# A DeltaNet and SwiGLU kernel: an order planned anew from other durations of computing steps

## The chip, the core and the metric

The kernel runs on one core of a Trainium2 chip, in fp32. A core has TensorE (PE: matmuls, with weight loads listed apart as PEld), VectorE (DVE), ScalarE (ACT), GpSimd (POOL), and SyncE (SP), which here issues nearly all DMAs. Matmul results go to eight PSUM banks of 128 partitions by 512 fp32 values. Counts of matmuls here are those of the profile, in which each fp32 matmul of the program is listed as two. The metric is the device time of one execution in microseconds. Before the change the median of 3 runs is 671.55 us (670.78 to 674.18).

## What is computed

Attention in the form of DeltaNet, then a root-mean-square norm and a SwiGLU feed-forward layer (FFN). There are 4 batches of 8 heads, 768 positions, head width 48; the FFN has 3072 tokens, width 384 and inner width 1536.

```python
k_n = k / (np.linalg.norm(k, axis=-1, keepdims=True) + 1e-06)
for t in range(S):                               # 768 steps
    kt, vt, bt = k_n[:, :, t], v[:, :, t], beta[:, :, t, None]
    y[:, :, t] = np.einsum('bhd,bhde->bhe', q[:, :, t], state)
    v_old = np.einsum('bhde,bhd->bhe', state, kt)
    state = state + bt[:, :, :, None] * np.einsum('bhd,bhe->bhde', kt, vt - v_old)
...
x = y.transpose(0, 2, 1, 3).reshape(B * S, H * D)
xn = x / np.sqrt(np.mean(x * x, axis=-1, keepdims=True) + 1e-06) * rms_g
g = xn @ w_gate
val = xn @ w_val
return (g / (1.0 + np.exp(-g)) * val) @ w_out
```

The weights arrive as float64 and are converted on the chip; the rest is fp32.

## The kernel before

**Tiling and stages.** The 768 positions are cut into 12 chunks of 64. Within a chunk the recurrence is solved for all 32 heads at once: a triangular system is inverted, and the state is carried from chunk to chunk. A chunk's 256 tokens (64 positions of 4 batches) then go through the norm and the FFN. For each chunk c there are these stages, by the names of the functions:

- `load`: q, k and v from DRAM by SP. For chunks from 2 on q comes in sixteen pieces.
- `norms`: lengths of k's rows (ACT, then DVE L729 and L730, POOL L731, DVE L734 and L735).
- `qpart`: q transposed, then products with k. In chunks 0 and 1 the transposition is done by PE; from chunk 2 on by one DVE instruction over 128x1024 (`square_turn`, L715). `scores` (L704) is 64 matmuls on 64 rows and 64 columns, into two banks; DVE masks them into pt (L765).
- `prep16` (chunks 0 and 1) and `invert` (from chunk 2 on): the inverse. `invert` reads products of k from DRAM into at (SP), scales them by beta (DVE L1023), sets up (ACT `start` L1028, `start2` L1034; DVE L1048, L1053, L1058), and does 15 steps of two DVE instructions each (L1070 and L1076), in which each needs the one before it. Then `spread` (ACT L1093, POOL L1096) and DMAs. `prep16` does the same for 16-wide blocks in 7 steps (L903 and L909).
- `recur`: state products (L1199, L1210), the difference from v (DVE L1246), the inverse times it (L1281, L1295, L1307, L1317; `u` is written by ACT L1349 and DVE L1351), the new state (L1404, DVE L1355), y (DVE L1439), the norm (ACT L1429, POOL `root` L1452 to L1455). From chunk 4 on y goes through DRAM and is transposed by DVE (L1473); before that by PE (L1483). DVE L1510 and L1522 form sums of xf.
- the FFN: chunks 0 and 1 by `ffn_plain` (up L1558, down L1540), the rest by `ffn` and `down`, which save multiplications: 30 groups of 8 matmuls up (L1651), each read from its bank by ACT (L1663) or added by DVE (L1661); Silu (ACT L1667) and a DVE product (L1668); then `down` with DVE sums (L1700), seven groups of 12 matmuls (L1708), and DVE and ACT to read them (L1713, L1717).

The conversion of the 18 pieces of weights (ACT, then DVE L607, L610, L615, L639) takes place in the first 100 us, beside chunks 0 to 2.

**Who sets the order.** All instructions are first listed as `Op`s by `P.add(engine, duration, function, priority, r=, w=, ...)`. The duration is a number in us in the source, such as `1.0` or `V(n) = 0.13 + 0.0011 * n`. `Plan.forward` then lays the operations out on five engines from these durations (it also has terms for banks, DMA service, and the supply of instructions); `backward` gives each one its latest start; `shake` shifts priorities at random, from one number. `run` does `rounds` plain rounds and then one for each number in `MOVES`, and keeps the order whose planned end is the earliest. The operations are issued in that order, so it is fixed in the program:

```python
        for k in range(rounds + len(MOVES)):
            order = self.forward([t for t, _ in free], until if filler else 0.0)
            ...
            if best is None or self.end < best[0]:
                best = self.end, [(op, op.start) for op in order]
            if k >= rounds - 1:
                if k < rounds + len(MOVES) - 1:
                    self.shake(MOVES[k - rounds + 1])
                continue
            self.backward()
            self.reorder()
```

Each shake builds on the state that the one before it left. In planned gaps of PE before 70 us, `filler` puts matmuls of the identity into a spare bank (L1826), with 1, 2 or 4 blocks of 128 columns each. Banks are handed out in the planned order too. On the chip an engine takes its instructions in the program's order and waits by semaphores for other engines.

Of the kernel before, what the change touches and what calls it, by code (L numbers as in the profile page):

```python
# [25 lines left out]
ROUNDS, MOVES = (8, 3), (8000067, 8000597, 8000948, 8001017, 8002724, 8006360, 8008220, 8019300, 8029128, 8041120, 8046040, 8061420, 8103060, 8171660, 8171980, 8172520, 8176051, 8186548, 8187777, 8188940, 8197021, 8197169, 8200311, 8221546, 8225628, 8270861, 8283640, 8284428, 8285760, 8285870, 8288410, 8295221, 8301729, 8305291, 8310247, 8324080, 8458740, 8499977, 8522895, 8527737, 8540674, 8542770, 8573880, 8576584, 8577340, 8579620, 8580620, 8594840, 8603040, 8637560, 8655411, 8656870, 8664720, 8672920, 8873930, 8885129, 8893086, 8956398, 8960108, 9314698, 9382016, 9442358, 9601943)  # L26
BLOCK, ASKED, LACKED = 256, 140, 193
REACT, TURN, LAND = 2.4, 3.45, 2.6
STICK = 1.0
# [315 lines left out]
def kernel(  # L345
# [17 lines left out]
    nc = tc.nc  # L363
# [21 lines left out]
    half = sbt("half", [128, 16])  # L385
# [44 lines left out]
    AK = [("acc", 0), ("acc", 1)]  # L430
# [17 lines left out]
    ms = sbt("ms", [128, 2, 2], 2)  # L448
    rs = sbt("rs", [128, 2], 2)
# [333 lines left out]
    def prep16(c):  # L783
        pr = 8.0 if c == 1 else 0.0
        pd = pr + (1 if c else 0)
        pi = (1.0, 45.0)[c]
        i2, ikq = c, c
# [10 lines left out]
        psf = Group()  # L798
# [57 lines left out]
        ab = [("ab", c, n) for n in range(4)]  # L856
        ak = [("acc", c)]
# [15 lines left out]
                nc.scalar.copy(flat(side)[:, L * c : L * c + 33 * 15 + 1 : 33], share())  # L873

        P.add("ACT", 0.6, start, pd, r=["half"], w=ak)
        P.add("ACT", 0.4, start2, pd + 0.5, r=[psf], w=ak, last=psf)
        x, xkeys = x16[c], [("xs", c)]
        diag = a16[c].rearrange("p j t -> p (j t)")[:, 1 : 1 + 34 * 7 + 1 : 34]
        pair = x.rearrange("p i t -> p (i t)")[:, 0:128].rearrange("p (j k) -> p j k", k=L // 2)
# [17 lines left out]
        for j in range(0, L - 2, 2):  # L897
            n, m = j + 2, L - 2 - j

            def step(j=j, n=n, m=m):  # L900
                old, new, lo = (3, 0, 1) if j % 4 else (0, 3, 0)
                cols = slice(L * c + j + 2, L * c + L)
                nc.vector.tensor_tensor(  # L903
                    out=acc[:, 1:3, 0:n, cols].rearrange("p a i t -> p i a t"),
                    in0=sides[old][:, 0:n, j : j + 2, None].to_broadcast([128, n, 2, m]),
                    in1=a16[c][:, None, j : j + 2, j + 2 : L].to_broadcast([128, n, 2, m]),
                    op=ALU.mult,
                )
                nc.vector.tensor_reduce(  # L909
                    out=acc[:, new, 0:n, cols],  # L910
                    in_=acc[:, lo : lo + 3, 0:n, cols].rearrange("p a i t -> p i t a"),
                    axis=AXL.X,
                    op=ALU.add,
                )

            P.add("DVE", 0.47 + 0.0052 * n * m, step, pi, r=ab, w=ak)

        xflat = x.rearrange("p i t -> p (i t)")

# [5 lines left out]
                else:  # L925
                    nc.vector.tensor_copy(out=dst, in_=src)

        P.add("ACT" if c else "DVE", 0.97 if c else 0.55, spread, pi, r=ak, w=xkeys)
        P.add("DVE", V(256), lambda: nc.vector.transpose(out=turned[1], in_=xflat), pi, r=xkeys, w=["turn1"])
        psb = Group()  # L930

# [78 lines left out]
    def invert(c):  # L1010
        pd = due(c, 110) + 1
# [24 lines left out]
                        bt[rows, par : W : 2],  # L1036
                    )

        P.add("ACT", 1.0, start, pd, r=["half"], w=AK)
        P.add("ACT", 0.9, start2, pd + 0.5, r=bkeys, w=AK)  # L1040


# [22 lines left out]
        for j in range(0, W - 2, 2):  # L1065
            n, m = j // 2 + 1, W - 2 - j

            def step(j=j, n=n, m=m):
                old, new, lo = (3, 0, 1) if j % 4 else (0, 3, 0)
                nc.vector.tensor_tensor(  # L1070
                    out=acc[:, 1:3, 0:n, j + 2 : W].rearrange("p a i t -> p i a t"),
                    in0=acc[:, old, 0:n, j : j + 2, None].to_broadcast([128, n, 2, m]),
                    in1=at_[:, None, j : j + 2, j + 2 : W].to_broadcast([128, n, 2, m]),
                    op=ALU.mult,
                )
                nc.vector.tensor_reduce(  # L1076
                    out=acc[:, new, 0:n, j + 2 : W],
                    in_=acc[:, lo : lo + 3, 0:n, j + 2 : W].rearrange("p a i t -> p i t a"),
                    axis=AXL.X,
                    op=ALU.add,  # L1080
                )

            P.add("DVE", 0.47 + 0.0052 * n * m, step, pi, r=[("at", 0), ("at", 1)], w=AK)

        def spread(dst, op, turn):
            for side in range(2):
# [90 lines left out]
    def recur(c):  # L1177
# [245 lines left out]
        for h in halves:  # L1423
            gy = groups(psy, h)

            if c == 0:
                p = h[0]
                for g in range(2):
                    P.add("ACT", A(192) + 0.15, lambda p=p, g=g: nc.scalar.activation(  # L1429
                        out=xflat[:, 128 : 320], in_=psy[g, p].t[:, 192 * p : 192 * p + 192], func=ACTF.Square,  # L1430
                        scale=1.0 / math.sqrt(DM), accum_out=ms[i2][:, p, g : g + 1],
                    ), py, r=[psy[g, p]], w=[("x1", 1), ("ms", i2, p)], last=psy[g, p])
# [429 lines left out]
```

## Time and profile before

| What | Value |
|---|---|
| median of 3 runs | 671.55 us (670.78 to 674.18) |
| profiled execution | 673.21 us, of it span 671.5 us |
| mean granted clock of PE | 0.994 |
| matmuls and weight loads | 10070 each |
| L1651, all | 301.2 us busy, 276 and 277 ns each |
| L1661 (DVE) | 121.3 us, 180 times 683 ns |
| L1076, L1070 (DVE) | 70.9 and 52.7 us, 150 times each |
| L1028 (ACT, `start` of `invert`) | 10.4 us, 10 times 1041 ns |
| L715 (DVE, qt) | 12.4 us, 10 times 1238 ns |
| PE idle, 0 to 100 us of the span | 9.7 us |
| PE idle, 100 us to the end | below 1 us in the windows of 20 us |

Times are of one profiled execution. In the profile an engine's idle time ahead of a group is put down to the instruction that released it last. "PE bank L704 <- DVE qt L715" is time in which PE stood ahead of L704 and L715 on DVE, which writes qt, ended the wait. A row with "issue" is time for which the profile shows no cause. SPq is the time of SP's queue in issuing.

### The profile page before, as it was taken

The numbers are of one execution on the slowest core, as the hardware profiler recorded it, in microseconds if no ns is written. First come the engines' busy times: TensorE is split into PE (matmuls) and PEld (weight loads), VectorE is DVE, ScalarE is ACT, GpSimd is POOL, SyncE is SP. The second block draws the span as 40 slices with busy tenths as digits, with TensorE's granted clock in tenths as the row PEclk, the third lists the DMA queues.
The fourth block names the chain that finished last, engine by engine and source line by source line (L and its number), as shares of the span: only waits on it lengthen the run. The fifth ranks groups of instructions, "written<-read, shape, count | busy, mean of one in ns | idle before, by whom it ended". The sixth has DMA issues, their size and how long they took to land.

```text
span 671.5 us, 23512 instructions
## 1 busy us (share of the span) xinstructions
PE 657.3 (98%) x10070; PEld 608.2 (91%) x10070; DVE 577.0 (86%) x1199; ACT 298.2 (44%) x685; POOL 88.5 (13%) x105
## 2 busy tenths in 40 slices
PE   9899989999999999999999999999999999999997
PEld 6788768787799999999999999999999999999997
DVE  6999889999999998997998898899998798457472
ACT  7554343454235455355345345345345354343241
POOL 4212211050300040040031030030040010000000
PEclk9999979999999999999999999999999999999999
DMA  9483666573325336345347456476346434102100
GB/s 233 125 221 108 135 166 167 91 146 75 48 63 79 63 84 107 57 99 91 54 123 109 76 132 96 82 168 97 48 117 92 84 79 70 26 2 48 24 1 24
DMA packets 261822, 62.31 MB, mean 93 GB/s; under 512 B 248627, under 2 KB 253782, under 8 KB 261718
## 3 DMA queue, kind: packets, MB, share of 16 engines
q1 hardware_dynamic: 258438, 60.02, 45.5%
q8 instruction: 79, 1.29, 0.8%
q10 hardware_dynamic: 3280, 0.79, 0.6%
q14 instruction: 25, 0.20, 0.1%
HBM read 44.25 MB, written 16.52 MB: 91 GB/s over the span
## 4 chain that ended last, share of the span: by engine, by line
PE 79%; DVE 12%; SPq 3%; DMA 2%; issue 2%; ACT 1%; POOL 1%; DVEq 0%; POOLq 0%
PE bank L1651 36%; PE bank L1708 19%; PE bank L1558 7%; PE bank L1540 4%; PE bank L704 3%; PE bank L1199 3%; SPq L487 3%; PE bank L1281 1%; PE bank L1317 1%; DVE tmp L1661 1%; DVE acc L1076 1%; PE bank L685 1%; PE bank L1404 1%; PE bank L1124 1%; DVE acc L1070 1%
## 5 line engine op out<-in xcount | busy, mean ns | idle before, releaser
L1651 PE MATMUL bank<-xf,w_in 128*128 128x128 f32 x1440 | 177.4, 276 | 0.0
L1651 PEld LDWEIGHTS bank<-xf,w_in 128*128 128x128 f32 x1440 | 168.7, 192 | 0.8
L1661 DVE TENSOR_TENSOR tmp<-tmp,bank 128x512 f32<-128x512 f32 x180 | 121.3, 683 | 34.6 <-PE bank L1651 30.2
L1651 PE MATMUL bank<-xf,more 128*128 128x128 f32 x960 | 123.8, 277 | 0.0
L1651 PEld LDWEIGHTS bank<-xf,more 128*128 128x128 f32 x960 | 115.1, 192 | 0.9
L1663 ACT COPY tmp<-bank 128x512 f32<-128x512 f32 x120 | 69.0, 584 | 63.0 <-PE bank L1651 49.4
L1667 ACT ACTIVATE tmp<-tmp 128x256 f32<-128x256 f32 x120 | 50.1, 417 | 93.7 <-DVE tmp L1661 93.2
L1076 DVE TENSOR_REDUCE acc<-acc 128x30 f32<-128x90 f32 (+4 forms) x150 | 70.9, 472 | 5.2
L731 POOL TENSOR_TENSOR knrm<-ksum,half 128x16 f32<-128x16 f32 x12 | 35.5, 2960 | 274.5 <-DVE ksum L730 274.5
L1708 PE MATMUL bank<-wo_sb,hf 128*128 128x192 f32 x360 | 63.8, 329 | 0.0
L1708 PEld LDWEIGHTS bank<-wo_sb,hf 128*128 128x128 f32 x360 | 58.1, 190 | 0.5
L1070 DVE TENSOR_TENSOR acc<-acc,at 128x60 f32<-128x60 f32 (+4 forms) x150 | 52.7, 351 | 2.4
L1668 DVE TENSOR_TENSOR hf<-tmp 128x256 f32<-128x256 f32 x120 | 49.0, 418 | 5.5 <-ACT tmp L1667 4.7
L1540 PE MATMUL bank<-wo_sb,hf 128*128 128x384 f32 x96 | 35.2, 506 | 0.0
L1558 PE MATMUL bank<-xf,w_in 128*128 128x256 f32 x144 | 34.6, 387 | 0.0
L1558 PE MATMUL bank<-xp,w_in 128*128 128x256 f32 x144 | 33.4, 383 | 0.0
L1558 PEld LDWEIGHTS bank<-xp,w_in 128*128 128x128 f32 x144 | 26.8, 190 | 4.6 <-DVE more L1616 0.2
L1558 PEld LDWEIGHTS bank<-xf,w_in 128*128 128x128 f32 x144 | 26.4, 190 | 4.4 <-issue 0.2
L1713 ACT COPY tmp<-bank 128x192 f32<-128x192 f32 x30 | 9.5, 316 | 41.7 <-PE bank L1708 41.2
L1540 PEld LDWEIGHTS bank<-wo_sb,hf 128*128 128x128 f32 x96 | 18.3, 196 | 9.9 <-issue 0.6
L1096 POOL COPY acc<-acc 128x128 f32<-128x128 f32 x40 | 18.8, 500 | 63.1 <-DVE acc L1076 62.8
L1510 DVE TENSOR_TENSOR xf<-xf 128x256 f32<-128x256 f32 (+1 forms) x70 | 24.7, 381 | 2.5 <-ACT xf L1475 1.9
(198 smaller groups left out, 985.8 us busy)
## 6 DMA issues: line engine op xcount, KB each, us to landing
at<-dkk SPq DMA_DIRECT2D x20, 256.0 KB, 3.7
more<-in_moe_w_gate_dram SPq DMA_DIRECT2D x6, 768.0 KB, 7.6
vt<-in_v_dram SPq DMA_DIRECT2D x24, 192.0 KB, 4.0
k<-in_k_dram SPq DMA_DIRECT2D x23, 192.0 KB, 4.2
out_dram<-tmp SPq DMA_DIRECT2D x46, 96.0 KB, 2.2
more<-in_moe_w_val_dram SPq DMA_DIRECT2D x5, 768.0 KB, 8.4
more<-in_moe_w_out_dram SPq DMA_DIRECT2D x5, 768.0 KB, 5.5
dyn<-yn SPq DMA_DIRECT2D x16, 192.0 KB, 2.0
```

The source lines that it names most:

```text
L731: P.add("POOL", 2.95, lambda: nc.gpsimd.tensor_tensor(out=knrm[i2], in0=ksum[i2], in1=half, op=ALU.pow), pn, r=[("ksum", i2), "half"], w=[ ...
L1070: nc.vector.tensor_tensor(out=acc[:, 1:3, 0:n, j + 2 : W].rearrange("p a i t -> p i a t"), in0=acc[:, old, 0:n, j : j + 2, None].to_broadc ...
L1076: nc.vector.tensor_reduce(out=acc[:, new, 0:n, j + 2 : W], in_=acc[:, lo : lo + 3, 0:n, j + 2 : W].rearrange("p a i t -> p i t a"), axis=A ...
L1510: P.add("DVE", V(128 * n), lambda dst=dst, a=a, b_=b_, op=op: nc.vector.tensor_tensor(out=dst, in0=a, in1=b_, op=op), pxv, r=[("xp", 0)], ...
L1540: nc.tensor.matmul(po[p].t[:, 0:DM], hf[:, spot(f), 128 * p : 128 * p + 128], wo_sb[:, spot(f)], start=(f == f0), stop=(f == f1 - 1), skip ...
L1558: nc.tensor.matmul(ps.t[:, TOK * side : TOK * side + TOK], w_in[:, side, h_, 3 * t + i_, n : n + 128], x_[:, 2 * t : 2 * t + 2].rearrange( ...
L1651: nc.tensor.matmul(g.t[:, 128 * z : 128 * z + 128], fac[:, side, 128 * f : 128 * f + 128], xf[:, xs], start=(begin and z == 0), stop=False ...
L1661: P.add("DVE", V(512), lambda t=t, g=g: nc.vector.tensor_tensor(out=t, in0=t, in1=g.t, op=ALU.add), -1, r=[g], w=[tk], last=g)
L1663: P.add("ACT", A(512), lambda t=t, g=g: nc.scalar.copy(t, g.t), -1, r=[g], w=[tk], last=g)
L1667: P.add("ACT", A(256), lambda t=t: nc.scalar.activation(out=t[:, 0:256], in_=t[:, 0:256], func=ACTF.Silu), -1, w=[tk])
L1668: P.add("DVE", V(256), lambda t=t, f0=f0, p=p: nc.vector.tensor_tensor(out=hf[:, spot(f0) : spot(f0) + 2, 128 * p : 128 * p + 128], in0=t[ ...
L1708: nc.tensor.matmul(g.t[:, 0:192], a_[:, f], b_[:, f], start=(begin and f == 0), stop=(f == 5), skip_group_check=True)
```

## The change

Seven lines with durations of computing steps, the seed of the plain rounds (8 to 21) and their number (3 to 16), and the list of moves (63 to 92 numbers, none in common). No instruction's operands, shape or engine is changed, and no duration of a transfer. The number of instructions of each kind is the same on all engines but for the fillers.

```diff
-ROUNDS, MOVES = (8, 3), (8000067, 8000597, 8000948, 8001017, 8002724, ...
+ROUNDS, MOVES = (21, 16), (21000076, 21000207, 21000651, 21003860, 21005160, ...
...
         P.add("ACT", 0.6, start, pd, r=["half"], w=ak)
-        P.add("ACT", 0.4, start2, pd + 0.5, r=[psf], w=ak, last=psf)
+        P.add("ACT", 0.3, start2, pd + 0.5, r=[psf], w=ak, last=psf)
...
-            P.add("DVE", 0.47 + 0.0052 * n * m, step, pi, r=ab, w=ak)
+            P.add("DVE", 0.37 + 0.0052 * n * m, step, pi, r=ab, w=ak)
...
-        P.add("ACT" if c else "DVE", 0.97 if c else 0.55, spread, pi, r=ak, w=xkeys)
+        P.add("ACT" if c else "DVE", 0.75 if c else 0.42, spread, pi, r=ak, w=xkeys)
...
-        P.add("ACT", 1.0, start, pd, r=["half"], w=AK)
+        P.add("ACT", 0.5, start, pd, r=["half"], w=AK)
         P.add("ACT", 0.9, start2, pd + 0.5, r=bkeys, w=AK)
...
-            P.add("DVE", 0.47 + 0.0052 * n * m, step, pi, r=[("at", 0), ("at", 1)], w=AK)
+            P.add("DVE", 0.37 + 0.0052 * n * m, step, pi, r=[("at", 0), ("at", 1)], w=AK)
...
             if c == 0:
                 p = h[0]
                 for g in range(2):
-                    P.add("ACT", A(192) + 0.15, lambda p=p, g=g: nc.scalar.activation(
+                    P.add("ACT", 0.33, lambda p=p, g=g: nc.scalar.activation(
...
-            P.add("POOL", 1.1, root, py, r=["half"], w=[(k_, i2, p) for p in h for k_ in ("ms", "rs")])
+            P.add("POOL", 1.1 if c else 0.7, root, py, r=["half"], w=[(k_, i2, p) for p in h for k_ in ("ms", "rs")])
```

The first three touched steps belong to `prep16` (chunks 0 and 1), the next two to `invert` (chunks 2 to 11), the last two to `recur` (`A(192) + 0.15` is 0.50).

More of the change, by code (lines that the diff above doesn't have):

```diff
@@ L25 @@
 OVERLAP = {"PE": 0.0, "ACT": 0.1, "DVE": 0.08, "POOL": 0.06, "SP": 0.0}
-ROUNDS, MOVES = (8, 3), (8000067, 8000597, 8000948, 8001017, 8002724, 8006360, 8008220, 8019300, 8029128, 8041120, 8046040, 8061420, 8103060, 8171660, 8171980, 8172520, 8176051, 8186548, 8187777, 8188940, 8197021, 8197169, 8200311, 8221546, 8225628, 8270861, 8283640, 8284428, 8285760, 8285870, 8288410, 8295221, 8301729, 8305291, 8310247, 8324080, 8458740, 8499977, 8522895, 8527737, 8540674, 8542770, 8573880, 8576584, 8577340, 8579620, 8580620, 8594840, 8603040, 8637560, 8655411, 8656870, 8664720, 8672920, 8873930, 8885129, 8893086, 8956398, 8960108, 9314698, 9382016, 9442358, 9601943)
+ROUNDS, MOVES = (21, 16), (21000076, 21000207, 21000651, 21003860, 21005160, 21018513, 21019060, 21169600, 21169769, 21174740, 21174873, 21177360, 21177620, 21179299, 21179347, 21179901, 21181160, 21181580, 21191792, 21304940, 21305080, 21305360, 21309320, 21309671, 21310500, 21310580, 21325833, 21332340, 21332420, 21356540, 21398369, 21398372, 21422500, 21422508, 21427278, 21427285, 21427691, 21427698, 21439489, 21439723, 21497890, 21497907, 21501920, 21501934, 21512331, 21512338, 21524824, 21524869, 21572401, 21572408, 21575674, 21575681, 21622738, 21622745, 21646850, 21646895, 21682364, 21682368, 21698110, 21698113, 21894795, 21894802, 21900501, 21900520, 21932080, 21932085, 21952540, 21952549, 21953502, 21953564, 22053106, 22053113, 22109200, 22109208, 22116442, 22116449, 22136020, 22136025, 22162400, 22162450, 22257428, 22257435, 22280690, 22280697, 22336083, 22336090, 22336809, 22336816, 22380012, 22380015, 22424385, 22424388)
 BLOCK, ASKED, LACKED = 256, 140, 193
```

## Prediction

> **What bounds the kernel now.** I read the page's busy shares first, then the windows by stage, then what TensorE (PE) waits for, then the chain of waits at the one place where it waits long, and last the timeline of the final chunk. From the page, busy time and share of each engine:
>
> ```profile
> PE 657.3 (98%) x10070; PEld 608.2 (91%) x10070; DVE 577.0 (86%) x1199; ACT 298.2 (44%) x685; POOL 88.5 (13%) x105
> ```
>
> PE sets the time: 14.2 us of 671.5 are all that an order could give back, apart from PE running slower. The windows (from:to, length, then busy time and number of instructions of PE, weight loads, DVE, ACT and POOL, then the granted clock, DMA share and GB/s):
>
> ```profile
> 0.00:20.00 20.00, 17.27 (x294) 12.80 (x296) 13.19 (x47) 14.62 (x25) 6.84 (x16) 1.00 0.84 199
> 20.00:40.00 20.00, 17.96 (x476) 15.70 (x475) 19.39 (x47) 10.47 (x26) 6.09 (x7) 1.00 0.72 197
> 40.00:60.00 20.00, 19.88 (x392) 16.77 (x387) 19.45 (x39) 11.13 (x22) 3.60 (x2) 1.00 0.58 134
> 60.00:80.00 20.00, 18.43 (x423) 14.96 (x422) 19.48 (x32) 8.37 (x16) 1.25 (x2) 1.00 0.53 124
> 80.00:100.00 20.00, 16.72 (x224) 12.78 (x226) 15.66 (x34) 8.45 (x20) 5.64 (x4) 0.83 0.69 176
> 100.00:120.00 20.00, 20.00 (x237) 16.36 (x227) 18.81 (x36) 6.29 (x15) 2.50 (x4) 1.00 0.66 152
> ```
>
> 9.7 us of PE's idle time lie in the first 100 us, where DVE is full from 20 to 80; behind that the windows are 20.00 busy but for 440:460 and 560:580 (19.93 and 19.56). There an order can only lose. And in 80:100 the granted clock is 0.83. What PE waits for (us in total, times, longest):
>
> ```profile
> PE bank L704 <- DVE qt L715: 3.3, 1, 3.3
> ...
> PE bank L1317 <- DVE u L1351: 0.9, 1, 0.9
> ...
> PE bank L1199 <- issue: 0.4, 1, 0.4
> ```
>
> One wait has 3.3 us. The chain of waits there (start, us, what):
>
> ```profile
> 79.43 3.12 DMA q<-in_q_dram
> 82.55 1.24 DVE at L1023
> 83.81 1.12 DVE acc L1048
> ...
> 89.23 1.26 DVE qt L715
> 90.48 0.04 issue
> 90.53 1.98 PE bank L704 x64
> 92.51 2.86 PE bank L1540 x4
> 95.37 1.44 PE bank L685 x8
> 96.80 2.59 PE bank L1558 x12
> 99.40 1.09 PE bank L704 x64
> ```
>
> The last load of chunk 2's q landed at 82.55, but DVE's transposition of q (L715) stood behind the inverse's scaling (L1023), its set-up and several of its steps, and ran at 89.23. PE had nothing from 87.25 to 90.53 (3.28 us). Then the same instructions are slower: 64 matmuls of L704 take 1.98 us, and 1.09 at 99.40. A finer window shows a granted clock of 0.51 from 90.5 to 96.5 and 1.00 behind it.
>
> **What the change does.** No instruction changes: it gives the planner other durations and other move numbers, so all that changes is the order on each engine, the bank that a group gets, and the filler matmuls (42 blocks of 128 columns in 19 instructions before, 38 in 20 after). The new durations are nearer to the trace (a step pair L1070 and L1076 takes 0.52 to 1.06 us, some 0.1 below the old plan) but for L1028, planned at 0.5 and measured at 1041 ns. The sum is taken from how the order of the built kernel stands against the old one.
>
> 1. *The wait and the slow clock go: -6.3.* In the new DVE order L715 of chunk 2 is row 150, ahead of both L1439, of L1023 (row 153) and of every inverse step; before it was row 168 with L1023 at 154. All sixteen q loads now stand ahead of the weight loads on SP, so q lands no later than 82.55 by this, and L715 may end at 83.8. PE has work to 87.25, and two groups of L1540 were moved ahead of L704, 1.3 us more. So 3.28 of waiting goes, and with it the half clock: (1.98 + 2.86 + 1.44) - (1.09 + 1.29 + 0.87, the same three at full clock elsewhere) = 3.03. Cover left: some 4.7 us; if q were later by more, the wait is back. What is queued behind L715 on DVE: the two L1439 (0.54 each) and the inverse, 1.24 later at its first step; its result is used by L1281 at 130.2, some 4 us behind the last load of it, so nothing waits.
>
> 2. *The first 87 us: +2.0 (bounds -2 to +4).* DVE is full there, and its order is changed from row 42 on: L779 and both L948 ahead of the norms' reductions, weight conversions earlier. PE's own order puts L1210, L1540, L1199, L1295 and L704 in a row, so two groups need banks whose readers have only just got the data: I price these at a reader's duration less what runs beside it, 0.7 and 0.8 (L765 takes 682 ns, L1246 546), and 0.5 for the rest. Lower end: half of the idle time of 20:80 (2.04 + 0.12 + 1.57 = 3.7) is recovered. Upper: as much again is added. The four filler blocks fewer run while PE is idle and cost nothing.
>
> 3. *Behind 100 us, new waits of PE: +5.0 (bounds 2.7 to 7).* Each by what DVE or ACT now does ahead of the needed step, less the slack that the step had.
>  - First chunk of the fast FFN form, L1708 at 222.35: the L1700 that it needs ended at 220.72, slack 1.6. Between the last L1661 and that L1700 DVE had 1.23 us of other work (one L765, one L1246), now 4.8 (two L765 at 0.68, two L1246 at 0.55, L1023 1.22, L1048 1.13): +3.6 - 1.6 = 2.0.
>  - L1708 at 521.56: L1700 ended at 520.54, slack 1.0; other work 2.34 before, 3.58 now, with one L715 more: 0.2.
>  - Around 150 us ACT's two L1093 (444 ns each) move from behind to ahead of the L1663 copies that empty PE's banks: 0.9.
>  - Last chunk: L1473 (0.97) now stands ahead of L1668 and L1700; before behind them, as the timeline shows (start, us, engine, line, what):
>
> ```profile
> 616.61 0.43 DVE L1668 TENSOR_TENSOR hf<-tmp 128x256 f32<-128x256 f32 x1 [0.48 <-ACT tmp L1667]
> 617.07 0.42 DVE L1700 TENSOR_TENSOR xp<-hf 128x256 f32<-128x256 f32 x1
> 617.19 2.11 PE L1708 MATMUL bank<-wsum,xp 128*128 128x192 f32 x12
> 619.00 0.97 DVE L1473 STREAM_TRANSPOSE xf<-yn 128x768 f32<-128x768 f32 x1
> ```
>
>    L1708 starts on the heels of L1700, so no slack: 1.0. If L1473's data were late too, DVE would stand still ahead of L1668, up to 2.2.
>  - These are 4.1. Many smaller moves are in nine more chunks that had no idle time to give: I add 0.9, the size of the largest such small wait (L1317). In three chunks DVE has less other work than before (0.97 against 2.1 to 3.5); PE did not wait there, so it gains nothing. The lower bound leaves out the 222 us item's half and the 0.9.
>
> 4. *Supply of instructions: +2.5 (bounds 0.4 to 3.3 for the runs named).* 10070 matmuls and as many weight loads fit q8 of the page's DMA queues (79 packets, 1.29 MB, 0.8% of 16 engines): 64 bytes each, 255 in a packet, and 0.008 x 16 x 671.5 / 79 = 1.09 us per packet. L704's 64 matmuls with their loads use up 128 in 1.09 us. Unbroken runs of such small matmuls reached 320 at most; the new order has one of 384 (L1199, L1295, L704, near 57 us) and one of 320 in a stage with a DMA share of 0.5 to 0.7, three packet borders. A packet late by its whole time costs 1.09; the one row that shows such a wait is L1199 <- issue at 0.4. I take 0.8 for each.
>
> 5. *Row counts: +0.4.* PE changes between 64-row and 128-row matmuls twice more (154 against 152 times); 12 L1708 take 2.15 us behind such a change and 1.95 otherwise, 0.2 each.
>
> Sum: -6.3 + 2.0 + 5.0 + 2.5 + 0.4 = +3.6 against the profiled execution's 673.2 us (span 671.5 and 1.7 outside it), 676.8. That execution is 1.7 above the median of 671.55; for the median the same sum gives 675.2.
>
> The Trainium skill bears on part 1 ("TensorE: Matmul & The Clock Gate", Part 1: The HAM clock gate): the clock is either full or half, and one activity window of some 3.4 us without work brings it to half. The trace agrees in kind: 3.28 us of idle, then 0.51. By that rule, in which the window is free-running, an idle stretch may or may not cover a window, so item 1's 3.03 could be only 0 in another run; by the row it is paid once.
>
> **Rivals.** *A new gap of PE of about 3 us (slower).* In the first 100 us DVE is 97% full, and a step that PE needs (L929 of chunk 1's inverse, L1351, L1355) that is moved back by a few conversions (L639, L615: under 1 us each) leaves PE with nothing for 3 us; then the clock halves again. It decides from an idle stretch of some 3 us in one piece: the waits of 1.4 us and less left the clock at 1.00 in 0:80. Price 6.3 on top of the sum: 681.5. For it: DVE's 19.4 of 20 and PE idle 1.57 in 60:80 already. Against it: the fillers, and that the longest of those idle pieces is 1.4. The skill's rule (same page and section) would set the same threshold; the trace has no idle stretch between 1.4 and 3.28 to test it.
>
> *Debits equal the credit (no change).* The four places shown (4.1) and 2.0 at the start, with 0.4 for supply and nothing else: -6.3 + 2.0 + 4.1 + 0.4 = +0.2, 671.8. For it: small waits may be absorbed by slack that I do not see, and the small items are the least shown. Against it: PE's 20.00 windows leave no slack once it has waited.
>
> *Faster.* The credit is kept and parts 3 and 4 come to under 1: -6.3 + 2.0 + at most 0.95 gives 668.2 or less; with nothing for them 667.3, and 665 if the start gains as well. For it: the credit is the only item seen whole in the trace, and the new durations are nearer to it. Against: the four places need DVE or ACT to do their rows in another order than the program has.
>
> That the change doesn't do what it says can be left out: L715's new row is in the built program.
>
> **Numbers.** A measurement of this kernel can't tell under 0.5% (3.4 us) from none: faster is below 668.2, slower above 674.9. The forecast, 675.2 with its own range 672 to 679, 0.50 (of it 0.31 above 674.9, 0.19 within); the new gap 0.21; debits equal credit 0.14; faster 0.15. So slower 0.31 + 0.21 = 0.52, same 0.19 + 0.14 = 0.33, faster 0.15. Range: down to 669, which leaves out most of the faster case (0.12), and up to 683, which takes in most of the new gap (0.06 left out).
>
> **What would show it.** Step 1: no wait L704 <- DVE L715 of 3 us, a clock of 1.00 in 80:100. Step 2: PE busy in 0:80 within 1 us of 73.5. Step 3: waits of L1708 on L1700 in the first fast chunk and in the last, windows behind 100 under 20.00. Step 4: "issue" rows at L1199, L1295 or L704. I am wrong if windows behind 100 stay at 20.00, if another window below 0.95 of the clock appears, or if the first 100 us hold over 12 us of idle.

## The result: 2.5% slower

| Kernel | Median | Span of the profiled execution | Mean granted clock |
|---|---|---|---|
| before | 672.46 us (670.78 to 674.18, 4 runs) | 671.5 us | 0.994 |
| after | 688.86 us (687.67 to 691.0, 4 runs) | 689.3 us | 0.991 |

The ratio is 1.0247, with an interval of 1.0207 to 1.0288. The forecast was 675.2, slower, so the sign was right and the size far too small: 16.4 us where 3.6 were expected, and above the range's end of 683. One profile of the experiments below, that of the first, is of an execution at a granted clock of 0.849, and its times are not used.

The busy row of the page and the windows of the kernel after (columns as before):

```profile
PE 662.7 (96%) x10072; PEld 610.8 (89%) x10072; DVE 574.4 (83%) x1199; ACT 296.3 (43%) x685; POOL 86.9 (13%) x105
```

```profile
0.00:20.00 20.00, 15.18 (x302) 11.82 (x302) 13.49 (x47) 15.28 (x25) 6.85 (x16) 1.00 0.84 199
20.00:40.00 20.00, 15.98 (x442) 14.02 (x438) 16.39 (x38) 9.66 (x24) 5.47 (x7) 0.97 0.64 177
40.00:60.00 20.00, 19.54 (x278) 15.69 (x276) 18.70 (x40) 9.50 (x20) 2.54 (x1) 0.94 0.56 114
60.00:80.00 20.00, 19.35 (x428) 16.85 (x428) 18.09 (x33) 8.53 (x15) 2.08 (x2) 0.91 0.57 147
80.00:100.00 20.00, 18.81 (x312) 14.50 (x311) 16.40 (x35) 8.46 (x22) 5.38 (x4) 1.00 0.79 193
100.00:120.00 20.00, 20.00 (x268) 16.60 (x266) 19.24 (x39) 6.52 (x13) 2.90 (x4) 1.00 0.49 105
...
180.00:200.00 20.00, 16.79 (x224) 14.73 (x224) 19.03 (x40) 4.61 (x9) 4.76 (x2) 0.91 0.29 58
200.00:220.00 20.00, 19.27 (x273) 18.70 (x272) 19.11 (x35) 12.38 (x30) 2.98 (x6) 1.00 0.36 56
220.00:240.00 20.00, 18.30 (x276) 16.82 (x275) 17.63 (x40) 4.97 (x16) 0.00 (x0) 1.00 0.36 62
```

The span grew by 17.8 us. PE's idle time went from 14.2 (671.5 - 657.3) to 26.6, which is 12.4 of it, and its busy time by 5.4. Of the idle time 9.7 lay in the first 100 us before and 11.1 now (100 less the five windows' sum); behind 100 us it went from 4.5 to 15.5. So 11.0 of the 17.8 are idle time in a stage that had none to give. The 5.4 of busy time are more than covered by one line: L1651's 2400 matmuls go from 301.2 to 307.3 us. Worked out by stretches of 40 us, one takes 122 to 125 ns in 180:300, where PE waits for DVE several times, and 115 to 118 in the same stretches before. Why is not shown: 8 in a row take 1.06 us and 16 take 1.95, so each start of a row of them counts some 0.17, and part of the stretch from 180 ran at the slow clock.

What PE waits for, in the kernel after:

```profile
PE bank L1651 <- DVE tmp L1661: 7.2, 10, 3.2
PE bank L848 <- issue: 3.4, 1, 3.4
PE bank L1708 <- DVE xp L1700: 2.3, 3, 1.5
...
PE bank L1199 <- DVE r L1242: 1.1, 1, 1.1
```

The L704 wait is gone. In its place are three kinds of waits: for DVE rows of the FFN, one without a cause in the profile ("issue"), and single waits ahead of 100 us. The largest sum is ten waits of the FFN's L1651 for the DVE instruction that reads its banks. The longest of these begins on DVE, some 18 us earlier. Its timeline (start, us, line, [idle before, and what ended it]):

```profile
169.79 1.01 DVE L1246 TENSOR_TENSOR r<-vt,bank 128x384 f32<-128x384 f32 x2
173.88 1.22 DVE L1023 TENSOR_TENSOR at<-at,beta_b 128x1024 f32<-128x1024 f32 x1 [3.08 <-DMA out_dram<-tmp]
...
189.59 0.54 DVE L1532 TENSOR_TENSOR tmp<-tmp,bank 128x384 f32<-128x384 f32 x1
190.05 0.41 DVE L1070 TENSOR_TENSOR acc<-acc,at 128x252 f32<-128x252 f32 x1
190.49 0.61 DVE L1076 TENSOR_REDUCE acc<-acc 128x126 f32<-128x378 f32 x1
191.01 1.47 DVE L1661 TENSOR_TENSOR tmp<-tmp,bank 128x512 f32<-128x512 f32 x2
```

and PE's at its end:

```profile
187.48 1.06 PE L1651 MATMUL bank<-xf,w_in 128*128 128x128 f32 x8
191.75 1.44 PE L1651 MATMUL bank<-xf,more 128*128 128x128 f32 x8 [3.21 <-DVE tmp L1661]
193.12 1.96 PE L1317 MATMUL bank<-u,pt 64*64 64x48 f32 x64
```

DVE stood still for 3.08 us ahead of L1023. The row names a store that landed then, but L1023 reads at, and SP's queue issued the two at loads at 166.66 and 170.21, between loads of mt and stores of the output; with the page's median of 3.7 us to landing the second is there at 173.9. Then DVE is full to 191. The L1661 that PE needs stands in the program behind nine of the inverse's step pairs, so PE gets its bank 3.21 us late, and 64 matmuls of L1317 then take 1.96 us instead of the 1.15 that they take elsewhere. Before, L1023 ran at 167.68 without waiting.

### The profile page after: what moved, and what is told of

Its sections match the earlier page's. It is cut to its first block, busy times and chain, and to the rows that moved or that the text cites. A ratio compares the mean times of both kernels' runs of the same rounds, so it can differ in the third digit from the quotient of the medians.

```text
span 689.3 us, 23506 instructions
## 1 busy us (share of the span) xinstructions
PE 662.7 (96%) x10072; PEld 610.8 (89%) x10072; DVE 574.4 (83%) x1199; ACT 296.3 (43%) x685; POOL 86.9 (13%) x105
## 4 chain that ended last, share of the span: by engine, by line
PE 49%; DVE 33%; DMA 6%; issue 5%; SPq 5%; ACT 1%; DVEq 0%; ACTq 0%
PE bank L1651 26%; PE bank L1708 13%; DVE tmp L1661 5%; SPq L487 5%; DVE acc L1076 5%; DVE acc L1070 3%; DMA q<-in_q_dram 2%; PE bank L704 2%; DVE hf L1668 1%; DVE more L1616 1%; PE bank L1199 1%; DVE xf L1510 1%; PE bank L1317 1%; PE bank L1281 1%; DVE ksum L729 1%
## 5 line engine op out<-in xcount | busy, mean ns | idle before, releaser
L1651 PE MATMUL bank<-xf,w_in 128*128 128x128 f32 x1440 | 180.8, 277 | 1.7 <-issue 0.8
L1651 PEld LDWEIGHTS bank<-xf,w_in 128*128 128x128 f32 x1440 | 170.1, 192 | 4.9 <-DVE tmp L1661 1.2
L1661 DVE TENSOR_TENSOR tmp<-tmp,bank 128x512 f32<-128x512 f32 x180 | 120.7, 681 | 41.0 <-PE bank L1651 33.9
L1651 PE MATMUL bank<-xf,more 128*128 128x128 f32 x960 | 126.5, 278 | 7.5 <-DVE tmp L1661 6.7
L1651 PEld LDWEIGHTS bank<-xf,more 128*128 128x128 f32 x960 | 115.4, 192 | 10.8 <-DVE tmp L1661 8.6
L1663 ACT COPY tmp<-bank 128x512 f32<-128x512 f32 x120 | 68.6, 584 | 75.3 <-PE bank L1651 52.9
L1076 DVE TENSOR_REDUCE acc<-acc 128x30 f32<-128x90 f32 (+4 forms) x150 | 70.9, 473 | 5.2
L1708 PE MATMUL bank<-wo_sb,hf 128*128 128x192 f32 x360 | 63.4, 327 | 0.1
L1708 PEld LDWEIGHTS bank<-wo_sb,hf 128*128 128x128 f32 x360 | 58.1, 190 | 0.4 <-DVE hf L1668 0.2
L1070 DVE TENSOR_TENSOR acc<-acc,at 128x60 f32<-128x60 f32 (+4 forms) x150 | 51.2, 342 | 2.2
L1540 PE MATMUL bank<-wo_sb,hf 128*128 128x384 f32 x96 | 34.3, 494 | 1.2 <-DVE hf L1566 1.2
L1558 PE MATMUL bank<-xf,w_in 128*128 128x256 f32 x144 | 34.2, 385 | 0.0
L1558 PE MATMUL bank<-xp,w_in 128*128 128x256 f32 x144 | 33.2, 381 | 0.0
L1558 PEld LDWEIGHTS bank<-xp,w_in 128*128 128x128 f32 x144 | 26.9, 190 | 4.7
L1558 PEld LDWEIGHTS bank<-xf,w_in 128*128 128x128 f32 x144 | 26.5, 190 | 4.3
L1540 PEld LDWEIGHTS bank<-wo_sb,hf 128*128 128x128 f32 x96 | 17.4, 190 | 10.9 <-DVE hf L1566 1.4
L1713 ACT COPY tmp<-bank 128x192 f32<-128x192 f32 x30 | 9.6, 320 | 38.3 <-PE bank L1708 36.6
L1565 ACT ACTIVATE tmp<-bank 128x256 f32<-128x256 f32 x24 | 9.2, 381 | 36.5 <-PE bank L1558 34.3
```

The source lines that it names most:

```text
L1070: nc.vector.tensor_tensor(out=acc[:, 1:3, 0:n, j + 2 : W].rearrange("p a i t -> p i a t"), in0=acc[:, old, 0:n, j : j + 2, None].to_broadc ...
L1076: nc.vector.tensor_reduce(out=acc[:, new, 0:n, j + 2 : W], in_=acc[:, lo : lo + 3, 0:n, j + 2 : W].rearrange("p a i t -> p i t a"), axis=A ...
L1540: nc.tensor.matmul(po[p].t[:, 0:DM], hf[:, spot(f), 128 * p : 128 * p + 128], wo_sb[:, spot(f)], start=(f == f0), stop=(f == f1 - 1), skip ...
L1558: nc.tensor.matmul(ps.t[:, TOK * side : TOK * side + TOK], w_in[:, side, h_, 3 * t + i_, n : n + 128], x_[:, 2 * t : 2 * t + 2].rearrange( ...
L1651: nc.tensor.matmul(g.t[:, 128 * z : 128 * z + 128], fac[:, side, 128 * f : 128 * f + 128], xf[:, xs], start=(begin and z == 0), stop=False ...
L1661: P.add("DVE", V(512), lambda t=t, g=g: nc.vector.tensor_tensor(out=t, in0=t, in1=g.t, op=ALU.add), -1, r=[g], w=[tk], last=g)
```

## Experiments

All times stand against the kernel before on the same chip (671.9 to 673.0 us in these batches). In the diffs, EDITS moves operations, named by number, to just behind (or, with a minus sign, ahead of) another one, in the finished order.

**Is the first term, L704's wait, there to be had?** Two runs hold pieces of chunk 2's inverse on DVE behind L715, in the order of before.

```diff
+EDITS = (((351, 354, 355, 356, 357, 358, 359, 360), 417),)   # L1023, L1048, L1058, L1053, four step pairs
```

> The order of before with one move: the inverse's eight first DVE pieces of chunk 2 (L1023 and its set-up, four step pairs) stand behind L715 and not ahead of it. Theory A (DVE, full to 240 us, is a second bound: what it loses early comes back as waits of PE): the wait of 3.28 us and the half clock in 80:100 are gone, but DVE is no earlier for it, so part of the 6.3 us comes back as waits of PE behind 100 us, 667.5 to 670 us. Theory B (PE's new waits come from the places of single rows in the new order): the whole credit shows, 665.5 to 667 us, and the windows behind 100 us stay at 20.00.

Measured: 677.32 us, ratio 1.0062 (1.0041 to 1.0084): longer than before, where both theories had it shorter.

```diff
+EDITS = (((351, 354, 355, 356, 357, 358, 359, 360), 335),)   # behind L715, L1566 and both L1522
```

> The order of before; the same eight pieces of chunk 2's inverse as in e1_q_first now stand behind L715, L1566 and both L1522, so that no FFN step stands behind them. The credit alone. If the wait and the half clock were worth 6.3 us by themselves: 666 to 667.5 us. If DVE is what sets the time there, some other wait on DVE takes their place: 670 to 674 us.

Measured: 676.58, ratio 1.0059 (1.0042 to 1.0077), longer than either case foresaw. DVE's and PE's waits:

```profile
DVE qt L715 <- DMA q<-in_q_dram: 5.2, 1, 5.2
```

```profile
PE bank L1199 <- DVE hf L1566: 3.9, 1, 3.9
```

With the inverse out of its way L715 still waits 5.2 us for q, whose last piece is issued behind a weight load on SP, and runs at 88.03 (89.23 before). So in the order of before it could not have run much earlier than it did. The longest wait of PE is at L1199 instead, and 2.2 us at L704 remain. The next two runs therefore move that load too.

```diff
+EDITS = (
+    ((410,), 412),            # the last q load, ahead of a v and a weight load
+    ((417,), 351),            # L715 just behind L1023
+    ((450,), 449),            # L1566 ahead of two step pairs
+    ((359, 360, 398), 450),
+)
```

> The kernel before, with its last q load of chunk 2 issued ahead of the v and wo loads, its DVE transposition L715 moved to just behind L1023, and L1566 moved ahead of the last two step pairs that stood ahead of it. If the q load's place behind the weight load was the cause of L715's lateness: no wait L704 <- DVE L715, clock 1.00 in 80:100, and 3.28 + 3.03 us less, less up to 2 us for the inverse's later steps: 666 to 668 against 672. If q lands late all the same (16 loads queue on one another), DVE stands still ahead of L715 for over 3 us and the time is 672 to 677, as in the two runs that only moved DVE rows.

Measured: 671.84 us, ratio 0.9995 (0.9979 to 1.001), no difference: between the two ranges named. The second run also moves L734 and L735 (`((398,), 397)`, and 359 and 360 alone behind 450):

> As e11_q_first_c, and L734 and L735 of chunk 2 (the reciprocal that GpSimd's L969 waits for) too are moved from behind the step pairs to just behind L715. In e11 the wait L704 <- L715 was gone, but 3.6 us later PE stood for 2.0 us at L685, which waits for L969, and the clock was 0.91 in 80:100; so of the expected 6.3 us only 0.6 came. If the two are one queue of late DVE rows: neither wait is over 0.5 us, the clock is 1.00 in 80:100, and the time is 667 to 669.5. If the next late row takes the place again, a new wait of PE of 1.5 us or more stands between 85 and 110, and the time is 671 to 673.

Measured: 672.94, ratio 1.0004 (0.9989 to 1.0019). PE's waits in the run with L715 moved, and in the run with L734 and L735 moved as well:

```profile
PE bank L685 <- POOL k L969: 2.7, 2, 2.0
```

```profile
PE bank L1540 <- DVE hf L1566: 3.2, 1, 3.2
...
PE bank L685 <- POOL k L969: 0.7, 1, 0.7
```

The gap goes from L704 (3.3) to L685 (2.0 near 90 us) and to L1540 (3.2 at 91). In these two and in the kernel before DVE has stood still for 2.3 to 4.0 us ahead of L1023 near 80 us, which waits for loads, and everything that PE needs next comes behind that. The row with the gap is only the one that happens to be last. So in none of these four orders did the 6.3 us come: 0.6 at most, in an interval that includes none.

**Does lateness of DVE early on make the later waits?** One run delays DVE in the kernel before, one relieves it in the kernel after, one changes PE's supply of instructions there.

```diff
-        P.add("DVE", V(256), lambda: nc.vector.transpose(...), pi, r=["turn0"], w=ab)
+        P.add("DVE", V(256), lambda: (c and [nc.vector.tensor_reduce(...) for _ in range(3)], nc.vector.transpose(...)), ...)
```

> The order of before, with three extra DVE reductions of 128x1024 (about 3.7 us together, worked out from L729's 0.94 us for 768) ahead of L865 of chunk 1 near 38 us; PE gets no extra work. Theory A: the time rises by all of it or more, 675 to 678 us. Theory B: DVE's slack hides most of it, below 673.5 us.

Measured: 681.06, ratio 1.0117 (1.0079 to 1.0155). 3.7 us of DVE work cost 9.0, more than theory A's range. PE's new idle time lies ahead of 100 us (the wait at L704 is 4.6 where it was 3.3, one at L1485 4.0 where it was 0.4), with a clock of 0.83 in 40:60 and 0.88 in 100:120 behind it. From 100 to 660 us PE's windows of 20 us are full but for 0.20, 0.11 and 0.51 us in three of them. So a late start alone does not make waits behind 180 us in the old order.

```diff
-                nc.vector.tensor_scalar(out=u, in0=u, scalar1=3, scalar2=None, op0=ALU.logical_shift_left)
+                pass
```

> The order of the changed kernel without the 18 shifts L607 of the weights' conversion (0.55 us each on DVE, 9.9 in all, in the first 150 us); the weights come out wrong. PE's instructions are the same, so L848's stall stays. Theory A: with DVE ahead, the waits of L1651 on L1661 fall from 7.2 to under 2.5 us, 674 to 681 us. Theory B: the waits stay, 685 to 690 us.

Measured: 683.87, ratio 1.0155 (1.0115 to 1.0196), with L607's 18 shifts of the weights' conversion left out. 5.0 less than the kernel after, but the L1651 waits for L1661 are still 6.4 (7.2 with the shifts), and PE's idle time behind 100 us is 15.1 (15.5). Early lateness (theory A) isn't their cause. What went lies elsewhere: the wait at L848 is 1.8 and not 3.4, and the clock is 1.00 in every window ahead of 680 us, where the slow clock of the kernel after costs some 5 us ((0.03 + 0.06 + 0.09 + 0.09) x 20 = 5.4).

```diff
-                    filler(fillers(pe, s))
+                    filler(FILL.get(op.n, fillers(pe, s)))
+FILL = {57: [4, 4], 61: [2], 189: [], 193: [2], 94: [4], 148: [4]}
```

> The order of the changed kernel with seven filler matmuls fewer ahead of 40 us (28 to 32 instructions with their weight loads), so that the packet of instructions for which L848 waited 3.37 us is needed later, behind L848 and L1485. Theory A: the stall and its half clock go (about 5), and with them DVE's delay and most of the waits of L1651 on L1661 behind 100 us: 676 to 681 us. Theory B: only the 5 go, 683 to 685 us. Theory C (the supply of instructions is the whole loss): near 672. If the stall only moves to another place, the time stays within 687 to 691 us and nothing is told.

Measured: 691.07, ratio 1.0265 (1.0212 to 1.0318). The trace lists 22 filler matmuls where it had 40, so nine of the program's 20 are gone, not seven. L848 waits no more, but L1558 waits 1.7 for L1489, and nothing is won.

**Is it a few rows, mended by hand?** Five moves in the kernel after put L1023 of three chunks behind rows whose data are there, and step pairs behind two of the L1661. Two step pairs of a late chunk then stand ahead of their set-up, so that chunk's inverse is another one.

```diff
+EDITS = (((878, 881, 882, 883), 583), ((890, 891, 892), 727), ((1112, 1115), 861),
+         ((2518, 2521, 2522, 2523), 2368), ((2530, 2531, 2532), 2370))
```

> The order of the changed kernel with five moves on DVE alone: in three chunks L1023 and its set-up stand behind rows that are ready while it waits for its load, and two times three step pairs behind two L1661. Theory B (single row places make the waits behind 180 us): the waits at 191.8, 234.8, 551.8 and 561.8 with the half clock behind the first go, some 8 us: 679 to 682 us. If the waits only move to the next group: 686 to 690 us.

Measured: 688.18, ratio 1.0232 (1.0206 to 1.0257). L1651's waits for L1661 fall from 7.2 to 3.4, and L1317 <- L1351 (2.1) and L1651 <- ACT L1663 (2.1) come up. Mending the rows with the longest waits (theory B) gives 0.7, less than the interval: the waits move, as the expectation's other case has it.

**The durations, or the list of moves?** Each half of the change alone:

```diff
-ROUNDS, MOVES = (21, 16), (21000076, ...      # the new durations with the old list
+ROUNDS, MOVES = (8, 3), (8000067, ...
```

> The new durations with the old seed, rounds and list of moves. Theory F (a list of moves lowers the planned end only for the durations for which it was found; with other durations it leaves an order that is hardly refined, full of small waits): slow as the changed kernel or slower, 685 to 700 us, waits of L1651 and L1708 on DVE in many windows behind 100 us. Theory E (the shorter durations put DVE's steps too tight, the list doesn't matter): near the changed kernel too, 685 to 692 us; e7 tells the two apart.

> The old durations with the new seed, rounds and list. Theory F: slow, 685 to 700 us, though the durations are the old ones. Theory E: with the old durations it is near before, 670 to 676 us.

Measured: new durations with the old list 691.98, ratio 1.0301 (1.0262 to 1.0339); old durations with the new list 685.48, ratio 1.0189 (1.0165 to 1.0213). Each half alone loses as much as both, or nearly. Two findings say how. The changed source with only the first of its 92 numbers gives the same program, instruction for instruction, on all five engines: the other 91 do nothing, none of them brings the planned end below the 672.5 that it has after the first. And the kernel before can be put in a like state:

```diff
-ROUNDS, MOVES = (8, 3), (8000067, 8000597, 8000948, ...
+ROUNDS, MOVES = (8, 3), (8000067,)            # in another run: the first 31 of the 63
```

> The kernel before, its own durations, with only the first of its list's moves: the order of its plain rounds. Theory F: as unrefined as the changed kernel's, so 683 to 692. If the list does little and the durations alone make the difference (theory E): 672 to 676.

> The kernel before with the first 31 of the 63 numbers of its list. With the first alone it took 687.5, with all 672.5. If the list's gain is spread over its moves (theory F): 676 to 684. If a few late moves make it (one place put right): 685 or above; if the first few do: 674 or less.

Measured: with the first number alone 687.51, ratio 1.0225 (1.0195 to 1.0254); with the first 31 677.24, ratio 1.0056 (1.0035 to 1.0078). With no change of durations, only the list's effect taken away, the kernel before is as slow as the kernel after (688.86), and half of the list brings back two thirds. So the list's gain is spread over its moves, as theory F has it. The waits with the first number alone are in other places than in the kernel after:

```profile
PE bank L1540 <- DVE hf L1566: 6.7, 2, 6.2
...
PE bank L1708 <- DVE xp L1700: 4.7, 3, 2.8
```

**Can the new durations do as well with a list of their own?** The finished order is put in as data: two orders refined for the new durations, from other random starts, and two for the old ones in the same way.

```diff
+ORDER = """16:0.000 ..."""
+def edit(best):
+    return best[0], [(known[int(n)], float(s)) for n, s in rows]
```

> The changed kernel's durations, but with an order that was refined for them: the same plain order to start from, and then 1638 moves of the same kind as those of the list, each kept because it did not lengthen the plan that these durations give. Theory F (the list of 91 moves that follows the first does nothing for these durations, so the changed kernel's order is hardly refined; the durations themselves are not at fault): back to the level of before, 668 to 676. Theory E (the shorter durations leave rows too little room, so any order made with them meets waits behind 180 us): stays at 683 or above, with waits L1651 <- DVE and L1708 <- DVE of 2 us or more. Between 676 and 683 both share.

> As the run beside it, with another start (other random draws) and 2376 kept moves. Theory F: 667 to 675. Theory E: 683 or above. If the two refined orders lie over 6 us apart, the order found by chance counts for more than either theory says.

> The durations of before, but not its list: another start and 1072 moves refined afresh for these durations, as was done for the new durations in the two refined runs (which came to 681.6 and 684.2). Theory E (the shorter durations cost the rest: an order refined with them has less room): with the old durations a fresh refinement lands near before, 671 to 676. Theory H (any freshly refined order lands at about 682, because what it is refined for is a plan and not the chip; the list of before was one of many and a good one on the chip): 679 to 686.

> As the run beside it, with other draws and 3986 kept moves, and a plan that comes out some 2 us longer than that one's. Theory E: 672 to 678. Theory H: 680 to 688.

Measured, in this order: new durations 681.59 (1.0145, 1.011 to 1.018) and 684.2 (1.0174, 1.0144 to 1.0204); old durations 681.18 (1.0116, 1.0093 to 1.0139) and 677.62 (1.0071, 1.0051 to 1.0092). Refining brings back 7.3 and 4.7 of the 16.4 us, less than theory F asks; the first lies where both theories share, the second in theory E's range. The old durations, refined afresh, don't get back to 672.5 either: one lies in theory H's range and one in theory E's, and the order with the shorter plan of those two is the slower one on the chip. The two pairs differ by 0.66% on average (4.4 us), with 0.3% and 0.45% between the orders of a pair, so these four times alone do not show a cost of the new durations.

The traces do, and the planner. A step pair (L1070 and L1076) costs DVE more when the next pair stands directly behind it. In the kernel after, for one shape (start, us):

```profile
187.52 0.44 DVE L1070 TENSOR_TENSOR acc<-acc,at 128x252 f32<-128x252 f32 x1
187.99 0.60 DVE L1076 TENSOR_REDUCE acc<-acc 128x126 f32<-128x378 f32 x1
188.62 0.42 DVE L1070 TENSOR_TENSOR acc<-acc,at 128x256 f32<-128x256 f32 x1
```

From the pair's start to the next row it is 1.10 us here, and 0.96 in the same chunk at 190.05, where L1661 stands behind the pair (lines above). The medians of the eight shapes are 0.54 to 1.09 with a pair behind and 0.46 to 0.97 with another row, 0.09 to 0.12 apart, in both kernels; some 60 of the 150 pairs have a pair behind them. The planner lets a DVE row begin 0.08 us ahead of the end of the one before it (`OVERLAP`), so for this shape the old number gives 1.05 and the new one 0.95. The new number is right for a pair with another row behind it, and 0.1 us or more too small for the others.

What that is worth can be worked out with the planner alone, held to the order that each program has. The table's first column is the planned end by the order's own durations. The second is the planned end by the new durations, with 0.12 us more for each step that directly follows another step on DVE and with 1.0 for L1028 (1.04 in the trace). The third is the measured time. All are differences in us from the kernel before (planned 666.3 and 666.5, measured on the same chip).

| Order | own plan | plan with the pairs' cost | measured |
|---|---|---|---|
| kernel after | +6.2 | +18.8 | +16.4 |
| new durations, old list | +12.7 | +21.8 | +20.1 |
| new durations, refined, first | 0.0 | +10.4 | +9.1 |
| new durations, refined, second | -0.9 | +8.5 | +11.7 |
| old durations, new list | +13.0 | +12.4 | +13.6 |
| old durations, first number | +13.3 | +12.6 | +15.0 |
| old durations, first 31 numbers | +4.6 | +5.5 | +4.3 |
| old durations, refined, first | +1.2 | +0.9 | +8.2 |
| old durations, refined, second | +3.4 | +3.8 | +4.7 |

With the pairs' cost eight of the nine come within 3.3 us of the measured difference; the first refined order of the old durations is 7.3 off, and why stays open. Two causes add up in the kernel after. Its order is worse by its own plan (6.2; its list does nothing), and its plan takes many pairs as shorter than they are (12.6 more); together that is 2.4 more than measured. The second moves the orders of the old durations by 0.9 at most, since the old number has room for it. This is worked out and fits the times; no run has the pairs' number put right and all else as in the kernel after.

One view tells where in time the loss lies: when DVE begins the scaling (L1023) of the last chunk's inverse. In the kernel before, the kernel after, the run with half the list and the run with its first number:

```profile
528.74 1.22 DVE L1023 TENSOR_TENSOR at<-at,beta_b 128x1024 f32<-128x1024 f32 x1
```

```profile
547.38 1.23 DVE L1023 TENSOR_TENSOR at<-at,beta_b 128x1024 f32<-128x1024 f32 x1 [2.64 <-DMA mt<-dx]
```

```profile
535.70 1.22 DVE L1023 TENSOR_TENSOR at<-at,beta_b 128x1024 f32<-128x1024 f32 x1 [0.69 <-DMA at<-dkk]
```

```profile
544.95 1.22 DVE L1023 TENSOR_TENSOR at<-at,beta_b 128x1024 f32<-128x1024 f32 x1 [2.98 <-DMA q<-in_q_dram]
```

From there to the end of the span it is 142.8, 141.9, 141.2 and 140.9 us, the same within 1.9. What these orders lose is lost by then. In the order of before this L1023 stands where its data have landed; in both unrefined orders DVE is held for 2.6 to 3.0 us by loads. But that wait is not the cause by itself: in the order mended by hand (688.18) and in the second refined one of the new durations (684.2) this L1023 waits for nothing, and begins at 546.91 and 543.07.

No run was measurably faster than the kernel before.

## Why the prediction was wrong, point by point

1. *The wait and the slow clock go, -6.3:* failed. The two signs named for it came true (no wait L704 <- L715, clock 1.00 in 80:100), but they are not the gain. "q lands no later than 82.55" was a misreading: that was the end of the wait ahead of L1023, put down to a q piece. The last piece came later: with the inverse behind it and not ahead, L715 ran at 88.03 in the old order, and in the kernel after it waits 2.9 for q and runs at 85.21. And a gap that is moved is not gone: with these rows moved in the old order the time was 0.6 us less at best and some 5 us more at worst. In the kernel after the slow clock is ahead of 80 us instead: (0.03 + 0.06 + 0.09) x 20 = 3.6 us of it, against 0.17 x 20 = 3.4 before, and 0.09 x 20 = 1.8 more near 192.
2. *The first 87 us, +2.0 (-2 to +4):* 3.5 by its sign, within its bounds but outside the 1 us that was named: PE is busy 70.05 us in 0:80 against 73.54. (DVE's 97% holds for 20:80; over the first 100 us it is 87%.)
3. *Behind 100 us, +5.0 (2.7 to 7):* the term that failed most; 11.0 of idle time and 6.1 in L1651 came. (By its own words its lower bound is 4.1 - 1.0 = 3.1.) The places named gave 2.3 (L1708 <- L1700 in the first fast chunk 1.7, where 2.0 was said, and 0.59 in the last, where 1.0 was said; nothing near 150 and at 521). The mechanism was right: DVE rows ahead of the one that PE needs. But the "many smaller moves" that got 0.9 were the bulk: ten waits of L1651 for L1661 alone are 7.2. Four places were priced in an order that was changed everywhere.
4. *Supply of instructions, +2.5:* 4.2 came in two "issue" rows (3.4 and 0.8), above its bound of 3.3, and the places were wrong: not L1295 or L704 but L848, from 34.7 to 38.08 us, and L1651. The DMA engines were full at the first of them, see below.
5. *Row counts, +0.4:* too small to be told from the rest.

Of the rivals, the new gap of PE came, twice (3.37 at L848, 3.21 at L1651), with a slow clock behind each (the first costs 0.39 x 4.4 = 1.7 us, where 3.03 was priced), but not by way of late conversions. Most of the loss is elsewhere.

Two steps lie behind these. The prediction left out what the new numbers do as a whole: that 91 of the 92 moves change nothing, and that the planned end of the new order is 672.5 against 666.3, could be seen before any run, and give +6.2 by themselves. And it read the new durations as "nearer to the trace", with the pair "some 0.1 below the old plan". That compares the rows' busy time with the number in the source. From start to start, which is what the planner's number stands for once its 0.08 is taken off, the old number is nearly right for the some 60 pairs that have a pair directly behind them, and with their cost the new order is planned 18.8 us longer than the old one; 16.4 was measured.

## What to carry to other kernels

A list of random moves belongs to the costs for which it was found: when a cost is changed, look first whether the list still changes the program, and compare the planned ends. Before a duration in a plan is lowered, measure it from start to start, and apart for each kind of row that can stand behind it. A planned order that is better by its plan need not be better on the chip; keep one because it was measured. And a long wait in the profile names the last late row, not the gain: before crediting it, ask what PE meets next when that row is early, and what held the engine of that row.

## What the runs showed of the hardware

**Instructions late behind a full DMA.** PE's timeline in the kernel after where L848 waits:

```profile
33.64 1.07 PE L848 MATMUL bank<-w_in 128*32 128x128 f32 x31
38.08 0.30 PE L848 MATMUL bank<-w_in 128*32 128x128 f32 x1 [3.37 <-issue]
```

and windows cut at the gaps and the slow clock (columns as above):

```profile
59.00:62.90 3.90, 2.79 (x83) 2.06 (x84) 3.88 (x7) 0.93 (x3) 1.61 (x1) 0.98 0.32 83
62.90:66.40 3.50, 3.50 (x97) 3.50 (x98) 1.75 (x5) 1.32 (x2) 1.48 (x1) 0.53 0.98 336
66.40:70.00 3.60, 3.60 (x74) 2.79 (x68) 3.53 (x6) 1.56 (x3) 0.00 (x0) 1.00 0.25 50
34.50:38.10 3.60, 0.23 (x8) 0.03 (x1) 1.48 (x5) 1.02 (x3) 1.38 (x3) 1.00 1.02 254
38.10:42.50 4.40, 4.40 (x16) 3.07 (x17) 3.14 (x11) 0.37 (x1) 0.00 (x0) 0.61 1.07 265
```

The fourth row is the gap: a DMA share of 1.02. PE stood for 3.37 us in the middle of a group of 32, three times the 1.09 that a packet of its instructions was taken to cost; in 30:42 two packets of that queue took 1.44 each (1.5% of 16 engines' 12 us). That the packet came late because weight loads filled the DMA engines fits this, and was not tested by itself. In seven of the other runs an "issue" wait of 1.8 to 3.2 us ends between 36.4 and 38.3 us too, ahead of L848, L1317, L1404 or L1826; but a full DMA is not enough, for the kernel before has a share of 0.92 to 1.26 from 34 to 40 us and no such wait. The prediction weighed the length of PE's runs of small matmuls and not the DMA share at that time. When the fillers were thinned out, this wait went, which agrees, but so did the plan's timing around it.

**The clock halves without a long gap.** The rows at 59 and 62.9: PE was idle for 1.11 us of 3.9, its longest wait 1.11 (L1199 for L1242), and the clock behind it was 0.53. The prediction's threshold of "some 3 us in one piece" is thus wrong. The Trainium skill ("TensorE: Matmul & The Clock Gate", Part 1: The HAM clock gate) names an idle window of about 3.4 us; the 3.37 and 3.21 us gaps come near that, this one does not. The same page of the Trainium skill says in its section "A second HAM failure mode: psum-queue depth-cycling" that frequent short idle times between groups of matmuls can throttle the clock too; whether this row, with one pause, is such a case is not shown. Nor is a long gap enough. In the run of the old durations with the new list, a gap of 3.23 us left the clock at 1.00 and one of 2.22 us halved it (two waits, then the windows that take in the end of each):

```profile
38.33 0.92 PE L1826 MATMUL bank<-ident 128*128 128x256 f32 x4 [3.23 <-issue]
551.82 1.98 PE L1651 MATMUL bank<-xf,more 128*128 128x128 f32 x8 [2.22 <-DVE tmp L1661]
```

```profile
39.00:42.00 3.00, 3.00 (x82) 2.77 (x81) 1.81 (x4) 0.86 (x2) 0.00 (x0) 1.00 0.68 120
551.50:555.00 3.50, 3.18 (x15) 3.18 (x16) 3.40 (x9) 0.42 (x1) 0.00 (x0) 0.57 0.00 0
```

**Late work can cost more than itself.** 3.7 us of DVE work in a stage where DVE is full cost 9.0 us. In the profiled executions PE's idle time rose by 6.3 us and its busy time by 2.2, with slow clocks behind the gaps.

**A step pair takes DVE longer when the next step stands directly behind it.** From start to start it is 0.54 to 1.09 us by shape with a step behind, and 0.46 to 0.97 with another row. Each step needs the one before it; that this is the reason is likely and not shown by itself.
